# Low parts of the second weights on VectorE, and result buffers in fixed turns, in an attention and mixture-of-experts kernel

## The chip, the cores and the metric

The program runs on one core of a Trainium2 chip. The metric is the device time of one execution in microseconds (us), the median of several executions. Engine names in rows: PE is TensorE (PEld its weight loads), DVE is VectorE, ACT is ScalarE, POOL is GpSimd, SP is SyncE, which issues most of the DMAs.

## The reference

Causal attention over 8 batches, 8 heads, 576 positions and a head width of 64, with a bias from cumulated scores, gives x with 4608 rows (tokens) of 512 numbers. A mixture of 8 experts follows. Each token goes to one expert, and the expert's two products are what the change is about:

```python
logits = x @ w_gate
e_idx = np.argmax(logits, axis=1)
...
for e in range(E):
    mask = e_idx == e
    ...
    h = np.maximum(x[mask] @ w1[e], 0.0)
    ye = h @ w2[e]
    out[mask] = gate_w[mask, None] * eom[mask, e, None] * ye
```

x, w1 (8 x 512 x 1024), w2 (8 x 1024 x 512) and the output are float32.

## The kernel before, in words

**Attention** takes the first 350 us or so. A planner (class `Order`, L97) orders its tasks on all engines by a table of places; the end of it also begins expert 0: the low parts of expert 0's second weights are already made there (L970 to L979), by GpSimd or VectorE as the planner chooses. The change does not touch that.

**The experts** follow one after another, e = 0 to 7. Numbers are split for the products: every operand is kept as a high part (a rounded copy, made by ScalarE) and a low part (what is left of it, made by a subtraction), and each product is three matmuls: high by high, high by low, low by high.

- `split_w1(f)` (L745) makes, for the next expert, the high part of a block f of the first weights on ScalarE (L740) and the low part on VectorE (L743, `w1l<-w1r,w1h`), 128x512 each. There are 8 blocks.
- `split_w2(f)` (L1026) makes the parts of block f of this expert's second weights: high on ScalarE (L726), low by `w2_lo` (L729) on GpSimd. There are 8 blocks.
- `gemm1` (L785, matmuls at L794) makes block f of the hidden layer in a PSUM bank pair `ph`, of which there are two; `relu` (L798) reads it twice: ScalarE writes the high part `hh` (L804), VectorE the low part `hl` (L806). Block f + 2 needs the bank pair of block f, so TensorE can't begin it before `hl` of block f is done.
- `product2` (L827, matmuls at L832) is the second product of one tile of 128 tokens, in bank `py` or `pf`. `result` (L1054) multiplies it by the token's weight on VectorE into a buffer `y` (L1057), and `scatter` has GpSimd issue an indirect DMA that writes the rows to the output (L1031).
- `gemm2_few` (L1068) does the same for a last tile of 32 or 64 tokens, in plain float32, with its own y (L1084).
- `ready` (L1087) turns 128 gathered tokens of the next expert: transposes on TensorE (L771, bank `pt`, two of them), high part on ScalarE (L775), low part on VectorE (L779).

The number of tokens of an expert is known only at run time. So `front(e, C)` (L1090), the first product and the tiles beyond the fourth, is written out for nine counts C (512, 544, ... 768) as the arms of a switch (expert 0 has eighteen), and each engine jumps to the arm that fits. `back(e)` (L1167), what all arms share, follows: results of the first tile, the remaining tiles, and the `ready` calls of the next expert in between. In this run experts 0 to 7 take the arms 544, 512, 512, 672, 704, 512, 576 and 640. Arms 544 and 672 have a short tile of 32 tokens, 576 and 704 one of 64.

Inside an arm each engine's order is set by the framework's scheduler from dependencies; in `back` it is the order of the code. A pool gives the buffers: a tag with bufs=3 is handed out in rotation, and a tile that is taken must wait until the last use of its buffer is over. All y tiles, also the short tile's, came from one tag with three buffers.

Of the kernel before, what the change touches and what calls it, by code (L numbers as in the profile page):

```python
# [9 lines left out]
F32 = mybir.dt.float32  # L10
# [7 lines left out]
P = 128  # L18
# [175 lines left out]
def moe_attention(ctx, tc, qk, v, s, idg, w1, w2, out):  # L194
    nc = tc.nc
# [532 lines left out]
    def w2_lo(f, eng):  # L728
        eng.tensor_sub(w2f("l", f), w2r[:, f], w2f("h", f).bitcast(F32))  # L729
# [147 lines left out]
    def hint(e):  # L877
        tc.switch_hint({g: regs[e] for g in ENGINES}, (1 if e else 2) * NA, f"expert{e}")
# [146 lines left out]

    def split_w2(f):  # L1026
        w2_hi(f)
        w2_lo(f, nc.gpsimd)

    def place(dst, ix, y):  # L1030
        ins = nc.gpsimd.indirect_dma_start(  # L1031
            out=dst, out_offset=bass.IndirectOffsetOnAxis(ap=ix, axis=0), in_=y, in_offset=None,
            bounds_check=dst.shape[0] - 1, oob_is_err=False)
        tc.declare_no_dep(ins.ins, group="out", reason="every token has one expert")
        tc.add_to_no_dep_group("out", ins.ins)
# [4 lines left out]
    def ybank(tag):  # L1040
        return pm.tile([P, DM], F32, tag=tag, name=tag, bufs=1)

    def gemm2(e, t, C, between=((),), tag="py"):

        m = min(P, C - t * P)
        p = ybank(tag)
        n = NF // len(between)
        for k, steps in enumerate(between):
            for step in steps:
                step()  # L1050
            product2(t, m, p, range(k * n, (k + 1) * n))
        result(e, t, m, p)

    def result(e, t, m, p):  # L1054
        y = mw.tile([P, DM], F32, tag="y", name="y", bufs=3)
        tb = tbs[e % 2]
        nc.vector.tensor_scalar_mul(y[0:m], p[0:m], tb[0:m, t, 2:3])  # L1057
        scatter(y, tb, t, m)
# [9 lines left out]
    def gemm2_few(t, m, tb):  # L1068

        G = P // m  # L1070
        W = DM // G
        ix = mw.tile([P, 1], I32, tag="ixf", name="ixf", bufs=2)
        nc.vector.tensor_scalar(ix, tb.bitcast(I32)[:, 1:2], float(G), grp[m], ALU.mult, ALU.add)
        hf = wt["hf"][:, :, 0:m]
        sl = slice(t * P, t * P + m)
        for fs in (slice(0, 6), slice(6, NF)):
            nc.gpsimd.tensor_add(hf[:, fs], wt["hh"][:, fs, sl].bitcast(F32), wt["hl"][:, fs, sl].bitcast(F32))
        p = ybank("py")
        for f in range(NF):
            for g in range(G):  # L1080
                nc.tensor.matmul(p[g * m:(g + 1) * m, 0:W], hf[:, f], w2r[:, f, g * W:(g + 1) * W],  # L1081
                                 start=(f == 0), stop=(f == NF - 1))
        y = mw.tile([P, DM], F32, tag="y", name="y", bufs=3)
        nc.vector.tensor_scalar_mul(y[:, 0:W], p[:, 0:W], tb[:, 2:3])  # L1084
        place(out.rearrange("n (g w) -> (n g) w", g=G), ix, y[:, 0:W])

    def ready(t, xg):  # L1087
        xcopy(t, xtrans(xg, pm.tile([P, ND, P], F32, tag="pt", name="pt")))

    def front(e, C, early=False):  # L1090


        nxt = e + 1 < E
        T = (C + P - 1) // P
        few = C % P if C % P in grp else 0
        if e == 0 and not early:
            for t in range(ET):
                ready(t, gather(tbs[0], t, xgs[t]))
        if T > LT:
            ready(LT, wt["last"])  # L1100
        c0 = min(ET * P, C - 256) if early else 0
        if few:
            places = few_places(e, T - 1, few)
        if nxt and e > 0:
            load_tab(e + 1)
        if early:
            for t in range(EY):
                scatter(banks["ye", t], tbs[0], t, P)

        ahead = range(2) if T > LT and C - c0 > 512 else ()  # L1110
        ph = {}

        def block(f):
            ph[f] = pm.tile([P, 2, 512], F32, tag="ph", name="ph")
            return ph[f]

        for f in ahead:
            gemm1(f, c0, C, block(f), 0)
        for f in range(NF):
            if f in ahead:  # L1120
                gemm1(f, c0, C, ph[f], 1)
            else:
                gemm1(f, c0, C, block(f))
            for part in "hl":
                relu(f, c0, C, ph[f], part)
            if e > 0:
                split_w2(f)
            if nxt:

                if e > 0 or not early:  # L1130
                    split_w1(f)
                elif f > 1:
                    split_w1(f - 2)
                if f < TMAX:
                    gather(tbs[(e + 1) % 2], f, xgs[f])
        if nxt and e == 0 and early:
            for f in range(NF - 2, NF):
                split_w1(f)
        if not few and nxt:
            run_all(load_w2(e + 1))  # L1140
        if nxt and e + 2 < E:
            run_all(load_w1(e + 2))

        tiles = ([] if e or early else list(range(EY))) + list(range(NC, T))
        if few:
            tiles.insert(0, tiles.pop())
        first = 0 if e else ET
        f0 = 3 if few else 0
        if f0:
            product2(first, P, firsts[e], range(f0))  # L1150
        for k, t in enumerate(tiles):
            if few and k == 0:
                gemm2_few(t, few, places)
                if nxt:
                    run_all(load_w2(e + 1))
            else:
                gemm2(e, t, C)
            if k + 1 < len(tiles):
                product2(first, P, firsts[e], range(f0, f0 + 1))
                f0 += 1  # L1160
        product2(first, P, firsts[e], range(f0, FB))
# [5 lines left out]
    def back(e):  # L1167

        if e == 0:
            where = {EY: (("hint", 0, 1), (2,), (3,), (4,))}  # L1170
        else:
            where = {1: ((),), 2: ((0,), (1,)), 3: (("hint", 2), (3,), (4,), ())}
        first = 0 if e else ET
        product2(first, P, firsts[e], range(FB, NF))
        result(e, first, P, firsts[e])
        for t, parts in where.items():
            gemm2(e, t, CMAX, tag="pf" if e and t == 2 else "py", between=[[(lambda u=u: hint(e + 1) if u == "hint" else ready(u, xgs[u])) for u in part
                                if e + 1 < E] for part in parts])

    rest = nc.values_load(rgi[0:1, 2 * E:2 * E + 1], min_val=0, max_val=E * NOV,  # L1180
# [13 lines left out]
    with tc.If(rest > 0):  # L1194
        for e in range(E):
            rv = nc.values_load(rgi[0:1, E + e:E + e + 1], min_val=0, max_val=NOV,
                                skip_runtime_bounds_check_because="counted by comparisons")
            run_all(load_w1(e))
            run_all(load_w2(e))
            with tc.For_i(0, rv, 1) as it:  # L1200
                tb = mw.tile([P, 1, 3], F32, tag="tbo", name="tbo")
                nc.sync.dma_start(tb, tab[bass.ds(it * P + (e * N + CMAX), P), :].unsqueeze(1))
                xg = sh.tile([P, DM], F32, tag=XGS[0], name="xg", bufs=1)
                nc.gpsimd.indirect_dma_start(
                    out=xg, out_offset=None, in_=xd,
                    in_offset=bass.IndirectOffsetOnAxis(ap=tb.bitcast(I32)[:, 0, 0:1], axis=0),
                    bounds_check=N, oob_is_err=False)
                p = pm.tile([P, ND, P], F32, tag="pt", name="pt")
                for c in range(ND):
                    nc.tensor.transpose(p[:, c, :], xg[:, c * P:(c + 1) * P], ident)  # L1210
                xt = sh.tile([P, ND, P], F32, tag=XGS[1], name="xto", bufs=1)
                nc.vector.tensor_copy(xt, p)
                ho = sh.tile([P, NF, P], F32, tag="kq", name="ho")
                for f in range(NF):
                    p = pm.tile([P, 2, 512], F32, tag="ph", name="ph")
                    for c in range(ND):
                        nc.tensor.matmul(p[:, 0, 0:P], w1r[:, c, f * P:(f + 1) * P], xt[:, c, :],
                                         start=(c == 0), stop=(c == ND - 1))
                    nc.vector.tensor_scalar_max(ho[:, f, :], p[:, 0, 0:P], 0.0)
                p = ybank("py")  # L1220
                for f in range(NF):
                    nc.tensor.matmul(p, ho[:, f, :], w2r[:, f], start=(f == 0), stop=(f == NF - 1))
                y = mw.tile([P, DM], F32, tag="y", name="y", bufs=3)
                nc.vector.tensor_scalar_mul(y, p, tb[:, 0, 2:3])
                scatter(y, tb, 0, P)

# [56 lines left out]
```

## Time and profile before

| what | value |
|---|---|
| median of 3 runs | 812.53 us (811.99 to 815.26) |
| the profiled execution | 817.58 us |
| its span | 815.7 us |
| mean granted TensorE clock | 0.983 |
| busy: PE, DVE, ACT, POOL | 95%, 56%, 51%, 48% of the span |

The profiled execution is one execution, 5.05 us above the median of the runs; what lies around its span is 1.9 us. A granted clock of 1.00 is 2.4 GHz and one of 0.50 is 1.2 GHz. In the timelines a row gives its start from the beginning of the span, its time, the line and tile, and in brackets how long the engine stood idle before it and what ended that.

### The profile page before, as it was taken

To read this page: it belongs to the slowest core of one execution; us is meant where nothing else is said; L and a number is where in the kernel's file an instruction comes from. 1 tells how busy PE (TensorE), PEld (TensorE's weight loads), DVE (VectorE), ACT (ScalarE), POOL (GpSimd) and SP (SyncE) were. 2 spreads that over 40 slices of the span, in tenths; PEclk is the share of its full clock that TensorE was granted. 3 is DMA by queue.
4 is the path that set the end of the run, shared out by engine and by line. 5 is a ranking of instruction groups with operands and counts; after the bars stand their busy time and mean duration, and the time that the engine had idled before them with its cause. 6 is when DMAs were issued, how large, how long until landed. Compare 5 with 4: busy or idle time off the path is not lost.

```text
span 815.7 us, 15604 instructions
## 1 busy us (share of the span) xinstructions
PE 775.3 (95%) x5121; PEld 618.9 (76%) x5121; DVE 452.8 (56%) x1265; ACT 412.5 (51%) x1125; POOL 389.1 (48%) x637
## 2 busy tenths in 40 slices
PE   4899999999999999969889999999999999999996
PEld 2577777777777777659767888898888878978985
DVE  5577878787878788845426345352372363443211
ACT  4788888888888888631315152430431241421300
POOL 4644575666665665554516345271281172541501
PEclk9999999999999999969989999999999999999999
DMA  8977787989897886240562715326125127223001
GB/s 216 247 194 205 208 231 228 239 222 223 239 236 221 202 210 130 52 166 2 146 227 68 260 55 192 124 78 227 56 78 200 68 80 249 71 63 131 14 29 43
DMA packets 71152, 125.03 MB, mean 153 GB/s; under 512 B 13978, under 2 KB 32540, under 8 KB 70942
## 3 DMA queue, kind: packets, MB, share of 16 engines
q1 hardware_dynamic: 62862, 100.75, 44.1%
q0 software_dynamic: 8080, 22.08, 8.5%
q8 instruction: 58, 0.95, 0.5%
q14 instruction: 152, 1.25, 0.5%
HBM read 103.12 MB, written 19.82 MB: 151 GB/s over the span
## 4 chain that ended last, share of the span: by engine, by line
PE 79%; DMA 6%; issue 5%; another core or an unknown queue 3%; DVE 3%; POOL 2%; SPq 1%; ACT 1%; POOLq 0%; DVEq 0%; ACTq 0%
PE ph L794 20%; PE py L832 11%; PE PT L435 10%; PE A L483 9%; PE S L380 8%; PE pf L832 8%; PE M L513 5%; PE S L383 3%; PE pt L771 2%; DMA cb<-cum 2%; PE A L481 1%; PE py L1081 1%; DMA con<-in_con_dram 1%; DMA xg<-xd,tbe 1%
## 5 line engine op out<-in xcount | busy, mean ns | idle before, releaser
L1031 POOL DMA_INDIRECT out_dram<-y,tb x34 | 33.5, 985 | 180.7 <-DVE y L1057 173.5
L794 PE MATMUL ph<-xh,w1h 128*128 128x512 f32 (+6 forms) x312 | 104.3, 334 | 4.8 <-DVE hl L806 3.1
L794 PE MATMUL ph<-xl,w1h 128*128 128x512 f32 (+6 forms) x312 | 103.3, 331 | 0.2 <-DVE xl L779 0.2
L794 PE MATMUL ph<-xh,w1l 128*128 128x512 f32 (+6 forms) x312 | 103.0, 330 | 0.0
L435 PEld LDWEIGHTS PT<-con,e 128*128 128x128 f32 x768 | 83.7, 142 | 14.7 <-issue 9.3
L775 ACT CAST xh<-pt 128x512 fp32r<-128x512 f32 x37 | 21.6, 587 | 144.0 <-PE pt L771 138.1
L435 PE MATMUL PT<-con,e 128*128 128x128 f32 x768 | 92.5, 276 | 1.5 <-ACT e L422 0.6
L380 PE MATMUL S<-kq 64*128 64x384 f32 (+3 forms) x512 | 82.3, 451 | 4.8 <-DVE pt L339 2.9
L483 PE MATMUL A<-pt,vraw 128*64 128x448 f32 (+3 forms) x640 | 84.8, 411 | 0.0
L743 DVE TENSOR_TENSOR w1l<-w1r,w1h 128x512 fp32r<-128x512 f32 x46 | 52.8, 1152 | 53.2 <-ACT w1h L740 53.0
L380 PEld LDWEIGHTS S<-kq 64*128 64x128 f32 x512 | 48.9, 189 | 37.5 <-issue 12.5
L832 PE MATMUL py<-w,hh 128*128 128x512 f32 x240 | 76.4, 400 | 0.0
L339 DVE COPY pt<-PT 128x384 f32<-128x384 f32 (+3 forms) x161 | 73.4, 503 | 3.3 <-PE PT L435 2.5
L483 PEld LDWEIGHTS A<-pt,vraw 128*64 128x64 f32 x640 | 44.9, 137 | 39.0 <-issue 29.7
L794 PEld LDWEIGHTS ph<-xh,w1h 128*128 128x128 f32 x312 | 59.1, 189 | 11.1 <-issue 5.0
L422 ACT ACTIVATE e<-pbB,m 128x128 f32<-128x128 f32 (+1 forms) x128 | 64.6, 506 | 1.8 <-DVE m L394 1.6
L806 DVE SCALAR_TENSOR_TENSOR hl<-ph,hh 128x512 fp32r<-128x512 f32 (+6 forms) x72 | 50.3, 701 | 27.0 <-ACT hh L804 26.9
L729 POOL TENSOR_TENSOR w<-w2r,w 128x512 fp32r<-128x512 f32 x45 | 57.9, 1300 | 13.7 <-ACT w L726 7.2
L740 ACT CAST w1h<-w1r 128x512 fp32r<-128x512 f32 x48 | 29.7, 621 | 68.3 <-issue 53.7
L794 PEld LDWEIGHTS ph<-xl,w1h 128*128 128x128 f32 x312 | 59.2, 190 | 3.8 <-DVE xl L779 1.1
L794 PEld LDWEIGHTS ph<-xh,w1l 128*128 128x128 f32 x312 | 59.0, 189 | 2.9
L337 ACT COPY pt<-PT 128x512 f32<-128x512 f32 (+2 forms) x95 | 51.9, 580 | 16.4 <-PE PT L435 15.1
(167 smaller groups left out, 1706.0 us busy)
## 6 DMA issues: line engine op xcount, KB each, us to landing
kq<-in_qk_dram SPq DMA_DIRECT2D x32, 576.0 KB, 5.3
cb<-cumd SPq DMA_DIRECT2D x31, 512.0 KB, 7.2
w1r<-in_moe_w_dram SPq DMA_DIRECT2D x7, 2048.0 KB, 10.6
w2r<-in_moe_w_dram SPq DMA_DIRECT2D x7, 2048.0 KB, 10.0
vraw<-in_v_dram SPq DMA_DIRECT2D x32, 320.0 KB, 3.4
cb<-cum SPq DMA_DIRECT2D x62, 160.0 KB, 6.7
xd<-x SPq DMA_DIRECT2D x32, 256.0 KB, 4.7
w1r<-in_moe_w_dram SPq DMA_DIRECT2D x4, 512.0 KB
```

Source lines behind the costliest of these rows:

```text
L337: nc.scalar.copy(out, in_)
L339: nc.vector.tensor_copy(out, in_)
L380: nc.tensor.matmul(d["s", t, j][:, 0:width(t)], qt[js, t * P:(t + 1) * P], kt[js, j * TL:j * TL + width(t)], start=True, stop=True)
L422: nc.scalar.activation(e[:, o:o + W], pbias(i, t, j), AF.Exp, bias=st[i].pop(("m", t, j)), scale=-1.0, accum_out=sums[i % 3][:, j, t:t + 1])
L435: nc.tensor.transpose(p[:, (c * len(g) + n) * P:(c * len(g) + n + 1) * P], st[i][etile(t, j)][:, o:o + P], ident)
L483: nc.tensor.matmul(p[j * D:(j + 1) * D, OB + q0:OB + S], vt[:, j, c, :], pt[:, c, j, q0:S] if c < NM else d["ptl"][:, (1 - j) * D:(2 - j) ...
L513: nc.tensor.matmul(p[:, n * 2 * G2:(n + 1) * 2 * G2], o, idgt[:, i % NPAIR], start=True, stop=True)
L729: eng.tensor_sub(w2f("l", f), w2r[:, f], w2f("h", f).bitcast(F32))
L743: eng.tensor_sub(w1f("l", f), w1r[:, :, f * P:(f + 1) * P], w1f("h", f).bitcast(F32))
L794: nc.tensor.matmul(p[:, u, 0:W], w1f(a, f)[:, c, :], wt[b_][:, c, us], start=(n == 0), stop=(n == 3 * ND - 1))
L806: nc.vector.scalar_tensor_tensor(lv, pv, 0.0, hv.bitcast(F32), ALU.max, ALU.subtract)
L832: nc.tensor.matmul(p[0:m], wt[a][:, f, sl], w2f(b_, f), start=(f == 0 and n == 0), stop=(f == NF - 1 and n == 2))
```

## The change

`split_w2` makes its low parts on VectorE. `result` no longer takes its buffer in rotation but from one of three tags of one buffer each, y0 to y2, by a number that the caller gives: 0 for an expert's first tile, 1 and 2 in turn for the tiles in an arm, 1, 2, 0 for those in `back`. The short tile's result goes to a buffer of attention (tag e0) that nothing else uses by then.

```diff
@@ -1025,7 +1025,7 @@
 
     def split_w2(f):
         w2_hi(f)
-        w2_lo(f, nc.gpsimd)
+        w2_lo(f, nc.vector)
 
     def place(dst, ix, y):
         ins = nc.gpsimd.indirect_dma_start(
@@ -1040,7 +1040,7 @@
     def ybank(tag):
         return pm.tile([P, DM], F32, tag=tag, name=tag, bufs=1)
 
-    def gemm2(e, t, C, between=((),), tag="py"):
+    def gemm2(e, t, C, between=((),), tag="py", slot=0):
 
         m = min(P, C - t * P)
         p = ybank(tag)
@@ -1049,10 +1049,10 @@
             for step in steps:
                 step()
             product2(t, m, p, range(k * n, (k + 1) * n))
-        result(e, t, m, p)
-
-    def result(e, t, m, p):
-        y = mw.tile([P, DM], F32, tag="y", name="y", bufs=3)
+        result(e, t, m, p, slot)
+
+    def result(e, t, m, p, slot):
+        y = mw.tile([P, DM], F32, tag=f"y{slot}", name="y", bufs=1)
         tb = tbs[e % 2]
         nc.vector.tensor_scalar_mul(y[0:m], p[0:m], tb[0:m, t, 2:3])
         scatter(y, tb, t, m)
@@ -1080,9 +1080,9 @@
             for g in range(G):
                 nc.tensor.matmul(p[g * m:(g + 1) * m, 0:W], hf[:, f], w2r[:, f, g * W:(g + 1) * W],
                                  start=(f == 0), stop=(f == NF - 1))
-        y = mw.tile([P, DM], F32, tag="y", name="y", bufs=3)
-        nc.vector.tensor_scalar_mul(y[:, 0:W], p[:, 0:W], tb[:, 2:3])
-        place(out.rearrange("n (g w) -> (n g) w", g=G), ix, y[:, 0:W])
+        y = sh.tile([P, 256], F32, tag="e0", name="yf", bufs=1)[:, 0:W]
+        nc.vector.tensor_scalar_mul(y, p[:, 0:W], tb[:, 2:3])
+        place(out.rearrange("n (g w) -> (n g) w", g=G), ix, y)
 
     def ready(t, xg):
         xcopy(t, xtrans(xg, pm.tile([P, ND, P], F32, tag="pt", name="pt")))
@@ -1154,7 +1154,7 @@
                 if nxt:
                     run_all(load_w2(e + 1))
             else:
-                gemm2(e, t, C)
+                gemm2(e, t, C, slot=1 + (k - bool(few)) % 2)
             if k + 1 < len(tiles):
                 product2(first, P, firsts[e], range(f0, f0 + 1))
                 f0 += 1
@@ -1172,9 +1172,9 @@
             where = {1: ((),), 2: ((0,), (1,)), 3: (("hint", 2), (3,), (4,), ())}
         first = 0 if e else ET
         product2(first, P, firsts[e], range(FB, NF))
-        result(e, first, P, firsts[e])
-        for t, parts in where.items():
-            gemm2(e, t, CMAX, tag="pf" if e and t == 2 else "py", between=[[(lambda u=u: hint(e + 1) if u == "hint" else ready(u, xgs[u])) for u in part
+        result(e, first, P, firsts[e], 0)
+        for n, (t, parts) in enumerate(where.items()):
+            gemm2(e, t, CMAX, tag="pf" if e and t == 2 else "py", slot=(n + 1) % 3, between=[[(lambda u=u: hint(e + 1) if u == "hint" else ready(u, xgs[u])) for u in part
                                 if e + 1 < E] for part in parts])
 
     rest = nc.values_load(rgi[0:1, 2 * E:2 * E + 1], min_val=0, max_val=E * NOV,
@@ -1220,7 +1220,7 @@
                 p = ybank("py")
                 for f in range(NF):
                     nc.tensor.matmul(p, ho[:, f, :], w2r[:, f], start=(f == 0), stop=(f == NF - 1))
-                y = mw.tile([P, DM], F32, tag="y", name="y", bufs=3)
+                y = mw.tile([P, DM], F32, tag="y0", name="y", bufs=1)
                 nc.vector.tensor_scalar_mul(y, p, tb[:, 0, 2:3])
                 scatter(y, tb, 0, P)
```

The instructions of TensorE, ScalarE and SyncE stay in the order they had. VectorE's order changes, since the scheduler places the eight new subtractions. In these rows w20 to w27 (w2l4, w2l5) are blocks 0 to 7 of the second weights and w1l0 to w1l3 pairs of blocks of the first weights.

VectorE at the start of the 512 arm of expert 1, before:

```order
L1186 BRANCH_PREFETCH_HINT
L743 TENSOR_TENSOR w1l0_5742<-w1r_78,w1h0_5741 128x512
L806 SCALAR_TENSOR_TENSOR hl_5935<-ph_11967,hh_5934 128x512
L743 TENSOR_TENSOR w1l0_5742<-w1r_78,w1h0_5741 128x512
L806 SCALAR_TENSOR_TENSOR hl_5935<-ph_11989,hh_5934 128x512
```

and with the change:

```order
L1186 BRANCH_PREFETCH_HINT
L729 TENSOR_TENSOR w20_5864<-w2r_79,w20_5864 128x512
L729 TENSOR_TENSOR w21_5918<-w2r_79,w21_5918 128x512
L729 TENSOR_TENSOR w22_5857<-w2r_79,w22_5857 128x512
L729 TENSOR_TENSOR w23_5912<-w2r_79,w23_5912 128x512
L729 TENSOR_TENSOR w2l4_5874<-w2r_79,w2h4_5873 128x512
L729 TENSOR_TENSOR w2l5_5868<-w2r_79,w2h5_5867 128x512
L743 TENSOR_TENSOR w1l0_5742<-w1r_78,w1h0_5741 128x512
L806 SCALAR_TENSOR_TENSOR hl_5935<-ph_11967,hh_5934 128x512
L729 TENSOR_TENSOR w26_5942<-w2r_79,w26_5942 128x512
L729 TENSOR_TENSOR w27_5890<-w2r_79,w27_5890 128x512
```

Six of the eight now stand ahead of the first `hl`, and two ahead of the second.

VectorE at the start of the 672 arm of expert 3, before:

```order
L1073 TENSOR_SCALAR ixf_19907<-tbf_19628,grp32_103 128x1
L779 TENSOR_TENSOR xl_5840<-pt_19621,xh_5839 128x4x128
L743 TENSOR_TENSOR w1l0_5742<-w1r_78,w1h0_5741 128x512
L806 SCALAR_TENSOR_TENSOR hl_5935<-ph_19631,hh_5934 128x672
L743 TENSOR_TENSOR w1l0_5742<-w1r_78,w1h0_5741 128x512
```

and with the change:

```order
L729 TENSOR_TENSOR w20_5864<-w2r_79,w20_5864 128x512
L779 TENSOR_TENSOR xl_5840<-pt_19621,xh_5839 128x4x128
L729 TENSOR_TENSOR w21_5918<-w2r_79,w21_5918 128x512
L729 TENSOR_TENSOR w22_5857<-w2r_79,w22_5857 128x512
L729 TENSOR_TENSOR w23_5912<-w2r_79,w23_5912 128x512
L729 TENSOR_TENSOR w2l4_5874<-w2r_79,w2h4_5873 128x512
L729 TENSOR_TENSOR w2l5_5868<-w2r_79,w2h5_5867 128x512
L729 TENSOR_TENSOR w26_5942<-w2r_79,w26_5942 128x512
L729 TENSOR_TENSOR w27_5890<-w2r_79,w27_5890 128x512
L1073 TENSOR_SCALAR ixf_19907<-tbf_19628,grp32_103 128x1
L743 TENSOR_TENSOR w1l0_5742<-w1r_78,w1h0_5741 128x512
L806 SCALAR_TENSOR_TENSOR hl_5935<-ph_19631,hh_5934 128x672
```

All eight stand ahead of the first `hl`. The 704 arm of expert 4 reads the same with its own widths; in the 576 arm of expert 6 seven and in the 640 arm of expert 7 all eight stand directly ahead of the first `hl`.

VectorE at the start of `back(0)`, with what each row waits for, before:

```order
L1057 TENSOR_SCALAR y_11848<-pf_6243,tb0_96 128x512 [waits DMASW6_49,DMASW7_49,DMASW2_49,PE_49]
L878 SWITCH_STRIDE
L878 ISA
L878 BRANCH_PREFETCH_HINT
L779 TENSOR_TENSOR xl_5840<-pt_11894,xh_5839 128x4x128 [waits Activation_49]
L779 TENSOR_TENSOR xl_5840<-pt_11901,xh_5839 128x4x128 [waits Activation_49]
```

and with the change:

```order
L1057 TENSOR_SCALAR y_11848<-pf_6243,tb0_96 128x512 [waits PE_49]
L878 SWITCH_STRIDE
L878 ISA
L878 BRANCH_PREFETCH_HINT
L779 TENSOR_TENSOR xl_5840<-pt_11894,xh_5839 128x4x128 [waits Activation_49]
L779 TENSOR_TENSOR xl_5840<-pt_11901,xh_5839 128x4x128 [waits Activation_49]
```

The order is the same; the first result no longer waits for three queues of GpSimd's DMAs (DMASW).

## Rows read from the trace of the kernel before

**Rows 1.** Page, part 1: TensorE's busy time, share of the span and instructions.
```profile
PE 775.3 (95%) x5121; PEld 618.9 (76%) x5121; DVE 452.8 (56%) x1265; ACT 412.5 (51%) x1125; POOL 389.1 (48%) x637
```

**Rows 2.** TensorE's timeline in expert 0's second half: start, us, line, operation, tile, [idle before].
```profile
416.89 0.40 PE L832 MATMUL py<-w,hl 128*128 128x512 f32 x1
...
421.30 1.11 PE L771 MATMUL pt<-con,xg 128*128 128x128 f32 x4 [4.01 <-DVE xl L779]
...
429.16 0.39 PE L794 MATMUL ph<-xh,w1h 128*128 128x512 f32 x1
```

**Rows 3.** VectorE's timeline, the same stretch.
```profile
411.48 0.35 DVE L1084 TENSOR_SCALAR y<-py,tbf 128x128 f32<-128x128 f32 x1 [1.19 <-PE py L1081]
...
419.90 0.75 DVE L1057 TENSOR_SCALAR y<-pf,tb 128x512 f32<-128x512 f32 x1 [8.07 <-DMA out_dram<-y,ixf]
```

**Rows 4.** Windows of 1 us: PE, PEld, DVE, ACT, POOL busy, PEclk, DMA share, GB/s.
```profile
419.00:420.00 1.00, 0.00 (x0) 0.00 (x0) 0.10 (x1) 0.00 (x0) 0.00 (x0) 0.72 1.05 406
...
423.00:424.00 1.00, 1.00 (x4) 0.73 (x3) 0.69 (x1) 0.09 (x1) 0.00 (x0) 0.50 0.58 229
...
426.00:427.00 1.00, 1.00 (x5) 0.81 (x4) 0.51 (x1) 0.46 (x1) 0.00 (x0) 0.87 0.09 25
```

**Rows 5.** Chain of work in order of time: start, us, engine, tile, line, count.
```profile
429.32 10.90 PE ph L794 x48
440.29 11.36 PE ph L794 x48
...
475.79 21.99 PE ph L794 x96
...
515.51 1.40 PE py L832 x6
517.35 1.39 PE py L832 x6
...
538.44 14.99 PE ph L794 x96
...
651.31 22.19 PE ph L794 x96
```

**Rows 6.** TensorE's timeline: the other three idle stretches behind VectorE after 421.30.
```profile
538.44 0.39 PE L794 MATMUL ph<-xh,w 128*128 128x336 f32 x1 [0.41 <-DVE hl L806]
...
610.41 0.40 PE L794 MATMUL ph<-xh,w1h 128*128 128x352 f32 x1 [1.39 <-DVE hl L806]
...
721.62 0.37 PE L794 MATMUL ph<-xh,w1h 128*128 128x288 f32 x1 [1.73 <-DVE hl L806]
```

**Rows 7.** VectorE's timeline in expert 4, one low part of a first weight.
```profile
605.76 3.70 DVE L743 TENSOR_TENSOR w<-w1r,w 128x512 fp32r<-128x512 f32 x1 [2.02 <-ACT w L740]
```

**Rows 8.** GpSimd's timeline beside it.
```profile
606.37 2.54 POOL L729 TENSOR_TENSOR w<-w2r,w 128x512 fp32r<-128x512 f32 x2
```

**Rows 9.** VectorE's timeline where experts 2, 3, 4, 6 and 7 begin.
```profile
475.83 0.75 DVE L1057 TENSOR_SCALAR y<-py,tb 128x512 f32<-128x512 f32 x1 [1.45 <-PE py L832]
479.08 0.69 DVE L743 TENSOR_TENSOR w1l<-w1r,w1h 128x512 fp32r<-128x512 f32 x1 [2.50 <-ACT w1h L740]
479.69 0.68 DVE L806 SCALAR_TENSOR_TENSOR hl<-ph,hh 128x512 fp32r<-128x512 f32 x1
...
525.36 0.21 DVE L1073 TENSOR_SCALAR ixf<-tbf,grp 128x1 int32<-128x1 int32 x1 [2.63 <-issue]
...
587.86 0.22 DVE L1073 TENSOR_SCALAR ixf<-tbf,grp 128x1 int32<-128x1 int32 x1 [2.42 <-issue]
...
701.07 0.21 DVE L1073 TENSOR_SCALAR ixf<-tbf,grp 128x1 int32<-128x1 int32 x1 [2.65 <-issue]
...
753.04 0.75 DVE L1057 TENSOR_SCALAR y<-py,tb 128x512 f32<-128x512 f32 x1 [1.45 <-PE py L832]
```

**Rows 10.** ScalarE's timeline where experts 2 and 7 begin.
```profile
473.90 2.18 ACT L726 CAST w<-w2r 128x512 fp32r<-128x512 f32 x4 [0.24 <-ACT xh L775]
...
753.44 1.14 ACT L726 CAST w<-w2r 128x512 fp32r<-128x512 f32 x2 [2.57 <-issue]
```

## The prediction, made before the changed kernel ran

> **What bounds the kernel now.** I read the page first: TensorE is busy for 95% of the span [rows 1], so only what shortens or lengthens its idle time can count. Then TensorE's timeline from expert 0's second half on, looking for idle stretches and what ended them. There are four behind VectorE: 4.01 us before 421.30 [rows 2], and 0.41, 1.39 and 1.73 us in experts 3, 4 and 6 [rows 6]. VectorE's own long waits elsewhere in `back` (some for a scatter, in experts 3 and 4) leave no gap on TensorE; they cost nothing.
>
> The 4.01 us begin with the y buffer. The short tile's result is made at 411.48 and scattered; expert 0's first result needs a buffer again and waits 8.07 us, to 419.90, until that scatter has landed [rows 3]. VectorE works in order, so the low parts of the gathered tokens stand behind it, their bank `pt` is not freed, and TensorE stops at 417.29 (416.89 plus 0.40). It then also loses its clock: 0.72 of full speed in the microsecond from 419, 0.50 at 423, 0.87 from 426 [rows 4]. Read as time at 1.2 GHz, that is from about 419.4 to 426.3.
>
> The three smaller stretches come from GpSimd. In expert 4 VectorE starts a low part of a first weight at 605.76 and takes 3.70 us [rows 7]; the same work takes 0.69 us elsewhere [rows 9]. GpSimd runs two subtractions from 606.37 to 608.91 [rows 8], and VectorE ends 0.55 us after them: it got nothing done beside them. `hl` stands behind that, and TensorE behind `hl`. The 512 arms show the same weakly: expert 1's first four blocks take 10.90 us, its last four 11.36; experts 2 and 5 take 21.99 and 22.19 for eight, against twice 10.90 [rows 5]. That is 0.46, 0.19 and 0.39 us.
>
> **The change, part by part.** *Fixed turns and the short tile's own buffer.* The first result of expert 0 waits for TensorE alone. What was held up from 417.1 on (the next issue after 416.89) are three steps of four transposes and six matmuls. At full clock a step takes 1.84 us (515.51 to 517.35) [rows 5], three take 5.5. Before, expert 1 began at 429.16 [rows 2], 12.06 us after 417.1. The gain is **6.5 us**: 4.0 of idle time, 2.5 of clock. What is late next is small: token parts are ready about as TensorE asks for them.
>
> *Low parts on VectorE.* Eight subtractions of 128x512 per expert, 56 in all. Back to back one takes 0.61 us (479.08 to 479.69) [rows 9], so 56 take 34 us. VectorE is idle 44% of the span, and the 1.3 to 3.7 us that first-weight parts take beside GpSimd fall to 0.69. In the middle of an arm this is hidden and the waits of rows 5 and 6 go. The cost is at the arm's start, where they stand ahead of the first `hl`; TensorE waits there when it comes to its third block.
>
> Expert 2 (512 arm): VectorE's last result ends at 476.58 (475.83 plus 0.75) [rows 9]. I take 0.24 us to enter the arm, as ScalarE shows there [rows 10]. Six parts, a first-weight part and `hl` follow: 476.8 plus 3.66, 0.61 and 0.68 is 481.8. The third block is due two blocks of 2.73 after 475.79, at 481.2; with 0.1 for the signal it waits 0.66 us. Later `hl` are in time. Net of what rows 5 give back: +0.47 in expert 2, +0.27 in expert 5, +0.20 in expert 1. Expert 1 has a second cost: it starts 6.5 us sooner, at 422.6, but its second weights are still loading; the DMA engines are at 0.58 in the microsecond from 423 and at 0.09 from 426 [rows 4]. That adds 0 to 1.6 us; I take 0.7, for most of the traffic is over by 424.
>
> Expert 3 (672 arm): VectorE enters late, at 525.36, with 2.63 us for which nothing is named [rows 9]. Ten instructions of 0.61 (the token part counted as one), 0.15 for the index and about 0.85 for a wider `hl` (estimate, from 0.68 for 512) end at 532.5. The third block starts 0.1 later, the fifth two blocks on. A block takes 3.68 (14.99 for four, less the last one's tail of 0.28) [rows 5]: 539.9 against 538.44 before [rows 6], **+1.5**.
>
> Expert 4 (704): from 587.86 [rows 9] the same to 595.1; four blocks of 3.85 (3.68 by width) bring the seventh to 610.5 against 610.41: +0.1. Its old stall of 1.39 is spent at the front. Expert 6 (576): from 701.07 [rows 9] seven parts and `hl` end at 706.1, five blocks of 3.15 later it is 721.95 against 721.62 [rows 6]: +0.3.
>
> Expert 7 (640) had no such work on VectorE. Its last result there ends at 753.79 [rows 9]. If it enters as ScalarE did, 2.57 us later [rows 10], eight parts and `hl` end at 762.1, and the third block, due at 760.0 (two blocks of 3.50), waits **2.1 us**. If it enters at once, ScalarE's high parts set the pace and nothing is lost. Late entry is what VectorE shows in the other three long arms, so I take 2.1.
>
> Nothing else moves on the path: the loads of the second weights can be issued sooner, the gathers too, and both have slack.
>
> **Sum.** -6.5 (expert 0) +0.9 (1) +0.5 (2) +1.5 (3) +0.1 (4) +0.3 (5) +0.3 (6) +2.1 (7) is **-0.8 us**: 816.8 against 817.58 for the profiled execution. That stands 5.05 us above the median; taken off, the median becomes **811.7**, which is no change, since about 0.5% (4.1 us) is what a measurement of this kernel can tell.
>
> **The rivals.** *Late entry in the 512 arms too (slower).* VectorE's entry there is hidden: its first row at 479.08 waited 2.50 us for ScalarE [rows 9], so entry may take anything up to that. If it takes 2.5, each front starts 2.3 us later: +6.8 over three arms, less the 0.7 that expert 1 has counted already: 811.7 plus 6.1 is 817.8. It decides from about 0.9 us of extra entry per arm. Against it speak ScalarE's 0.24 us in that arm and that it stands directly behind the switch; for it, 2.4 to 2.6 us in three of the seven. The Trainium skill, "Runtime: NRT & Kernel Launch", section "Instruction fetch mechanics", says that a taken branch to code outside the prefetched window must fetch it before going on; by that rule longer arms on VectorE, as here, would speak for this rival, and the trace agrees for the long arms and leaves the 512 arm open. Chance 0.15.
>
> *Entry is quick everywhere (faster).* If VectorE's late rows were not the jump, the parts would start some 2.5 us sooner in experts 3, 4, 6 and 7; then nothing is lost there and the 0.41, 1.39 and 1.73 us of rows 6 are won: -6.5 +1.7 (the 512 arms) -3.5 is -8.3, 804.2. Three like rows marked with no releaser speak against it. 0.08. Only expert 7 quick: -2.9, 809.6, still no change. 0.12.
>
> *The clock falls in a new wait.* By the sums above TensorE now waits 1.9 to 2.3 us at one place in each of experts 3, 4, 6 and 7. An idle stretch of 1.73 [rows 6] cost no clock; the one of 4.01 cost it about 2.1 us in, and then 6.9 us at half speed [rows 4]. A fall would cost up to 3.4: 815.1 for one, 818.5 for two. 0.14.
>
> *The change does not do what it says:* expert 0's result finds another wait, such as tokens or weights that land no sooner. Then the 6.5 stay: 818.2. The row's remaining wait names only TensorE, against it. 0.05.
>
> **How the numbers follow.** The forecast, with small errors of a term, has 0.40; 0.06 is for what I have not seen. Faster by over 0.5% (under 808.5) takes the quick entry and the low edges of the forecast and of expert 7: 0.20. Slower (over 816.6) takes late entry, the failed change and two falls of the clock: 0.23. The rest, 0.57, is no change. The range 806.0 to 818.5 leaves out most of the quick entry and the ends beyond two falls; the forecast's own is 809 to 814.
>
> **What would show it.** Right: no idle stretch of TensorE at 417 and a clock of 1.00 there; first-weight parts at 0.69 us throughout; a single wait of TensorE behind `hl` at the third block of each expert, about 0.7 us in the 512 arms and 2 us in the others, and none later. Wrong: waits of 2 us or more in the 512 arms, a clock of 0.50 inside an arm, no wait at all at third blocks, or the idle stretch in expert 0 still there.

## The result: slower by 0.8%, and where the time went

The changed kernel takes 820.39 us (median of 6 runs, 818.49 to 823.47) against 814.12 for the kernel before on the same chip: a ratio of 1.0083, 95% interval 1.0059 to 1.0107. A second comparison (below) gave 1.0105. The forecast was 811.7, its range ended at 818.5. In two of the four later sets of runs the kernel before took 834 and 840 us instead of 813 to 815, with expert 0's short tile at 430 to 441 us of the profiles instead of 408 to 414, so every ratio below is to the kernel before in the same set.

The short tile's result of expert 0 starts at 411.48 before [rows 3] and at 409.04 after. A second profile of the changed kernel has it at 413.54, so this difference is chance, and time is best counted from there, by the starts of VectorE's results `y`. To the last `y` of the kernel it is 396.9 us before and 405.5 after, 8.6 more (the second profile has 402.5, 5.6 more):

| stretch, us | before | after | difference | forecast |
|---|---|---|---|---|
| expert 0, short tile's result to last `y` | 17.9 | 17.6 | -0.3 | -6.5 |
| expert 1, last `y` to last `y` | 46.5 | 46.9 | +0.4 | +0.9 |
| expert 2 | 46.2 | 46.9 | +0.8 | +0.5 |
| expert 3 | 62.7 | 64.0 | +1.3 | +1.5 |
| expert 4 | 66.6 | 66.8 | +0.2 | +0.1 |
| expert 5 | 46.3 | 46.9 | +0.5 | +0.3 |
| expert 6 | 55.4 | 57.2 | +1.9 | +0.3 |
| expert 7, to its first `y` | 33.6 | 37.4 | +3.8 | +2.1 |

TensorE's busy time stays at 95% of a longer span; GpSimd's falls from 389.1 us [rows 1] to 314.0. The page after:

```profile
PE 777.2 (95%) x5121; PEld 622.0 (76%) x5121; DVE 455.0 (55%) x1321; ACT 412.3 (50%) x1125; POOL 314.0 (38%) x581
```

The larger group of low parts of first weights on VectorE follows, for the kernel before and then for the changed one (count | busy us, mean ns of one). The 0.69 us forecast for one is there; that part of the change works.

```profile
L743 DVE TENSOR_TENSOR w1l<-w1r,w1h 128x512 fp32r<-128x512 f32 x46 | 52.8, 1152 | 53.2 <-ACT w1h L740 53.0
```
```profile
L743 DVE TENSOR_TENSOR w1l<-w1r,w1h 128x512 fp32r<-128x512 f32 x46 | 32.1, 700 | 48.3 <-ACT w1h L740 48.3
```

TensorE's timeline after shows these idle stretches over 0.4 us: expert 0's, and one at the third block of each expert (experts 1 and 5 have the 0.71 of expert 2, and expert 3 has 1.53).

```profile
418.06 1.12 PE L771 MATMUL pt<-con,xg 128*128 128x128 f32 x4 [3.24 <-DVE xl L779]
...
479.62 0.47 PE L794 MATMUL ph<-xh,w1h 128*128 128x512 f32 x1 [0.71 <-DVE hl L806]
...
595.02 0.40 PE L794 MATMUL ph<-xh,w1h 128*128 128x352 f32 x1 [1.44 <-DVE hl L806]
...
706.46 0.40 PE L794 MATMUL ph<-xh,w1h 128*128 128x288 f32 x1 [2.04 <-DVE hl L806]
...
764.37 0.41 PE L794 MATMUL ph<-xh,w1h 128*128 128x320 f32 x1 [2.02 <-DVE hl L806]
```

The stretch of 4.01 us [rows 2] is still there, at 3.24, one of the prediction's own signs of being wrong. The others sit where the forecast put them, and the late waits of [rows 6] are gone. What the forecast's sum left out is in the windows (columns as in [rows 4]; PEclk is the third number from the end): the clock falls to 0.50 (1.2 of 2.4 GHz) in expert 0, and again after the waits of experts 6 and 7.

```profile
417.00:418.00 1.00, 0.00 (x0) 0.00 (x0) 1.00 (x3) 0.00 (x0) 0.31 (x1) 0.63 1.05 406
418.00:420.00 2.00, 1.94 (x7) 1.74 (x8) 0.73 (x3) 0.59 (x1) 0.69 (x1) 0.50 1.07 399
420.00:424.00 4.00, 4.00 (x13) 3.22 (x12) 1.26 (x2) 0.59 (x1) 0.00 (x0) 0.50 0.40 145
...
706.00:708.00 2.00, 1.54 (x9) 1.54 (x10) 2.00 (x5) 0.00 (x0) 1.59 (x2) 0.85 0.44 129
708.00:710.00 2.00, 2.00 (x10) 2.00 (x10) 1.00 (x2) 0.00 (x0) 1.50 (x2) 0.50 0.50 141
710.00:712.00 2.00, 2.00 (x14) 2.00 (x14) 0.00 (x0) 0.63 (x2) 1.51 (x2) 0.80 0.73 186
...
764.00:766.00 2.00, 1.63 (x9) 1.63 (x10) 1.05 (x2) 0.00 (x0) 0.00 (x0) 0.86 0.00 0
766.00:768.00 2.00, 2.00 (x10) 2.00 (x9) 0.00 (x0) 0.00 (x0) 0.00 (x0) 0.50 0.00 0
768.00:770.00 2.00, 2.00 (x13) 2.00 (x13) 0.00 (x0) 0.23 (x1) 0.00 (x0) 0.79 0.00 0
```

Expert 6 loses 0.30, 1.00 and 0.40 us of full clock in its three windows, 1.7 in all; expert 7 0.28, 1.00 and 0.42, again 1.7. These are the 1.6 and 1.7 by which both exceed their forecasts. In the second profile of the changed kernel only expert 7 of the two loses clock.

**Expert 0.** VectorE's timeline shows a wait of 7.28 us where 8.07 stood [rows 3], although the result now waits for no scatter:

```profile
409.04 0.35 DVE L1084 TENSOR_SCALAR yf<-py,tbf 128x128 f32<-128x128 f32 x1 [1.19 <-PE py L1081]
416.66 0.75 DVE L1057 TENSOR_SCALAR y<-pf,tb 128x512 f32<-128x512 f32 x1 [7.28 <-issue]
```

The rows of the sequencers (a q behind the engine's name; by line, with first and last start at the end) tell what the timeline doesn't: each engine's branch at the arm's end, and its first instruction behind it, a register load (L874) or, on SyncE, a move. The register loads wait for no semaphore.

```profile
L1279 SPq COMPARE_BRANCH  x2: 50/54/58, 409.5 to 416.5; - x2
L1279 SPq MOVE  x2: 38/40/41, 416.2 to 416.3; - x2
...
L1279 DVEq COMPARE_BRANCH  x1: 56/56/56, 409.1 to 409.1; - x1
L1279 POOLq COMPARE_BRANCH  x1: 49/49/49, 409.4 to 409.4; - x1
```
```profile
L874 DVEq TENSOR_LOAD <-rgi x1: 317/317/317, 416.2 to 416.2; - x1
L874 POOLq TENSOR_LOAD <-rgi x1: 317/317/317, 416.3 to 416.3; - x1
```

Three engines leave the arm between 409.1 and 409.5 and start behind it within 0.1 us of each other, some 7 us later (GpSimd's engine still works on the scatter until 410.7). In between, the queues that load instructions move nothing from 409 to 412, while the 4 MB of weights issued at the arm's end hold the DMA engines; then the packets of those queues run, and the engines go on. The DMA views of 409 to 412 and of 412 to 415 (packets, MB, share):

```profile
q1 hardware_dynamic: 227, 0.93, 93.7%
```
```profile
q1 hardware_dynamic: 266, 1.02, 94.2%
...
q14 instruction: 4, 0.03, 2.8%
q8 instruction: 1, 0.02, 2.2%
```

The same register load was in the trace of before, and the prediction did not read it:

```profile
L874 DVEq TENSOR_LOAD <-rgi x1: 314/314/314, 418.0 to 418.0; - x1
```

Before, then, VectorE was out of the arm at 418.3 only (418.0 plus 0.3), and the scatter held it from there to 419.90: 1.6 us of the 8.07.

### The profile page after: what moved, and what is told of

The parts are those of the page before. It is cut to its first block, busy times and chain, and to the rows that moved or that the text cites. A ratio compares the mean times of both kernels' runs of the same rounds, so it can differ in the third digit from the quotient of the medians.

```text
span 821.6 us, 15585 instructions
## 1 busy us (share of the span) xinstructions
PE 777.2 (95%) x5121; PEld 622.0 (76%) x5121; DVE 455.0 (55%) x1321; ACT 412.3 (50%) x1125; POOL 314.0 (38%) x581
## 5 line engine op out<-in xcount | busy, mean ns | idle before, releaser
L380 PEld LDWEIGHTS S<-kq 64*128 64x128 f32 x512 | 49.3, 191 | 39.8 <-issue 13.1
L804 ACT ACTIVATE hh<-ph 128x512 fp32r<-128x512 f32 (+6 forms) x72 | 43.7, 609 | 31.2 <-PE ph L794 26.9
L743 DVE TENSOR_TENSOR w1l<-w1r,w1h 128x512 fp32r<-128x512 f32 x46 | 32.1, 700 | 48.3 <-ACT w1h L740 48.3
```

What stands on the lines that cost most here:

```text
L380: nc.tensor.matmul(d["s", t, j][:, 0:width(t)], qt[js, t * P:(t + 1) * P], kt[js, j * TL:j * TL + width(t)], start=True, stop=True)
L743: eng.tensor_sub(w1f("l", f), w1r[:, :, f * P:(f + 1) * P], w1f("h", f).bitcast(F32))
L804: nc.scalar.activation(hv, pv, AF.Relu)
```

## The experiments

Theory J says that expert 0's wait is the jump out of the arm, slow because code is fetched while weights load, and that the scatter's wait runs beside it. Theory B, as predicted, says that it is the buffer. Theory Q says that in the other experts the loss is the place of the low parts ahead of the first `hl`; its rival W, that it is the work itself.

**The fixed turns alone.** The low parts go back: `w2_lo(f, nc.vector)` becomes `w2_lo(f, nc.gpsimd)` in `split_w2`.

> The fixed turns and the short tile's own buffer alone; the low parts stay on GpSimd. Theory J (VectorE and the sequencers of GpSimd and SyncE are held at the jump from the arm to the code behind it, whose code they must fetch while 4 MB of weights load): before, VectorE's register load behind that jump began at 418.0, so the buffer held the result only from 418.3 to 419.9, 1.6 us of the 8.07. The wait in front of expert 0's first result falls from 8.1 to about 6.5 us, TensorE's idle time behind it from 4.0 to 2.4 to 3.3 us with the clock still at 0.50 for some us, and the total is 1 to 2 us under before: 812 to 813, ratio 0.998 to 0.999. Theory B (the buffer was the whole wait, as predicted): no idle time and full clock there, 807.6, ratio 0.992.

811.65 us, ratio 0.9975 (0.9951 to 0.9999). In this profile the jump took 5.5 us (the short tile's result ends at 408.67, the register load starts at 414.1), TensorE was idle for 1.85 us, less than expected, and the clock still fell to 0.50. B falls, for its 0.992 lies outside the interval; J's 0.998 to 0.999 lies inside.

**The low parts alone.** The kernel before with `w2_lo(f, nc.vector)`.

> The low parts on VectorE alone; the result buffers rotate by three as before. Theory J: expert 0 is as before (4.0 us idle), all of the loss is in the arms, so this is the changed kernel plus the 1 to 2 us of the buffer: 820.5 to 822.5, ratio 1.008 to 1.010. Theory B: the changed kernel plus 6.5 is 827, ratio 1.016.

822.37 us, 1.0091 (1.0072 to 1.011): J's range again, and B's 1.016 lies outside. TensorE's idle time was 3.14 us, not 4.0.

**The kernel before, expert 0's loads behind the arm.**

```
     def front(e, C, early=False):
-        if not few and nxt:
+        if not few and nxt and e:
             run_all(load_w2(e + 1))
-        if nxt and e + 2 < E:
+        if nxt and e and e + 2 < E:
             run_all(load_w1(e + 2))
...
-                if nxt:
+                if nxt and e:
                     run_all(load_w2(e + 1))
...
     def back(e):
         first = 0 if e else ET
+        if e == 0:
+            run_all(load_w2(1))
+            run_all(load_w1(2))
         product2(first, P, firsts[e], range(FB, NF))
```

> The kernel before with one edit: the 4 MB of weights that expert 0's arm loads at its end are issued behind the arm, by the code that follows the switch. Theory J: with no load under way the jump takes about 2.5 us, as the entries into the long arms do (2.4 to 2.7 us with little traffic), the short tile's scatter lands sooner too, expert 0's first result starts by 415, TensorE is not idle at 417 and keeps a clock of 1.00: 6.5 us are won, of which expert 1 gives 0 to 3 back because its second weights land 4 to 6 us later; 807.5 to 811, ratio 0.992 to 0.996. Rival J2 (the jump takes its 6 to 7 us with or without traffic): the wait stays over 6 us, nothing is won, and the later weights cost 0 to 5 us; 814 to 819, ratio 1.000 to 1.006.

813.77 us, 0.9987 (0.9969 to 1.0004). For the total this is a miss of J, and J2's 1.000 lies inside the interval; the trace decides. VectorE's timeline and its register load:

```profile
411.29 0.35 DVE L1084 TENSOR_SCALAR y<-py,tbf 128x128 f32<-128x128 f32 x1 [1.19 <-PE py L1081]
418.91 0.75 DVE L1057 TENSOR_SCALAR y<-pf,tb 128x512 f32<-128x512 f32 x1 [7.27 <-DMA out_dram<-y,ixf]
```
```profile
L874 DVEq TENSOR_LOAD <-rgi x1: 318/318/318, 414.1 to 414.1; - x1
```

The jump fell to 2.5 us (411.64 to 414.1), so J2 falls. But now the buffer is the later of the two: 4.5 us from 414.4 to 418.9. The scatter did not land by 415; the weights issued behind the arm are under way with it.

**Both: the turns, and expert 0's loads behind the arm**, low parts on GpSimd.

> The fixed turns and the later loads together, low parts on GpSimd. Theory J: the buffer no longer matters when the scatter lands at once; within 1 us of the run with the later loads alone, ratio 0.992 to 0.996. If the buffer is what remains in that run, this one is 1 us or more faster than it. Rival J2: as the turns alone, or slower by the later weights, ratio 0.998 to 1.006.

811.17 us, 0.9957 (0.9941 to 0.9973), 2.6 us under the run without the turns. The two intervals just overlap, but the trace shows too that the buffer is what remained in that run. VectorE's timeline, its register load and TensorE's timeline:

```profile
412.58 0.75 DVE L1057 TENSOR_SCALAR y<-pf,tb 128x512 f32<-128x512 f32 x1 [3.25 <-PE pf L832]
```
```profile
L874 DVEq TENSOR_LOAD <-rgi x1: 320/320/320, 412.0 to 412.0; - x1
```
```profile
416.39 0.63 PE L771 MATMUL pt<-con,xg 128*128 128x128 f32 x4 [1.60 <-DMA out_dram<-yf,ixf]
```

Only with both gone does the result wait for TensorE. The clock is 1.00 throughout, and expert 0 takes 13.1 us. The packets of the instruction queues now run in 409 to 412, while little of the weights moves:

```profile
q1 hardware_dynamic: 156, 0.32, 55.3%
q8 instruction: 1, 0.02, 2.2%
q14 instruction: 2, 0.02, 1.7%
```

The edit moves less than its name says: SyncE, already behind the arm, issues one 2 MB load at 409.0, where the changed kernel issues one too, and the other at 409.5 instead of 407.5.

What is left of TensorE's idle time, 1.60 us, the row puts down to the short tile's scatter, and TensorE's sequencer agrees. GpSimd issues the scatter at 409.61, it lands 6.6 us later, and the last of the three semaphore instructions on the transposes' line (the last start, 416.3) stands right behind that:

```profile
409.61 1.03 POOL L1031 DMA_INDIRECT out_dram<-yf,ixf  x1 [1.42 <-DVE yf L1084]
...
out_dram<-yf,ixf POOLq DMA_INDIRECT x1, 6.6
...
L771 PEldq EVENT_SEMAPHORE  x3: 51/51/51, 410.2 to 416.3; - x3
```

In the kernel before and in the changed one the same row reads:

```profile
L771 PEldq EVENT_SEMAPHORE  x3: 51/51/51, 413.1 to 419.7; - x3
```
```profile
L771 PEldq EVENT_SEMAPHORE  x3: 51/51/51, 410.1 to 417.1; - x3
```

The scatter landed at 419.7 and at 417.0 there, and in all sixteen profiles the row stands within 0.05 us behind the landing. So three waits ran side by side: jump, buffer and TensorE's own for the scatter. Of the 4.01 us before, jump and buffer alone decided the last 1.5 (419.8 to 421.30). The rows do not tell which dependency makes TensorE wait for the scatter, and no run takes this wait away.

The jump in all profiles, from the end of the short tile's result to VectorE's register load, and expert 0's length:

| kernel | jump | result held by | TensorE idle | expert 0 |
|---|---|---|---|---|
| before | 6.2 | jump, then buffer | 4.01 | 17.9 |
| changed, two profiles | 6.9, 6.0 | jump | 3.24, 2.40 | 17.6, 15.3 |
| turns alone | 5.5 | jump | 1.85 | 15.0 |
| low parts alone | 6.0 | jump, then buffer | 3.14 | 16.3 |
| before, loads behind the arm | 2.5 | buffer | 3.24 | 16.2 |
| turns, loads behind the arm | 2.7 | neither | 1.60 | 13.1 |

The further profiles below agree: 5.3 us twice where the loads stay in the arm, 2.4 to 3.2 in seven where they don't.

**The low parts pinned.** The changed kernel, each low part kept behind what is written ahead of it on VectorE, the `hl` of its block.

```
-        eng.tensor_sub(w2f("l", f), w2r[:, f], w2f("h", f).bitcast(F32))
+        return eng.tensor_sub(w2f("l", f), w2r[:, f], w2f("h", f).bitcast(F32))
...
-        w2_lo(f, nc.vector)
+        tc.keep_in_program_order(w2_lo(f, nc.vector))
```

> The changed kernel with one edit: each low part of a second weight stands on VectorE right behind the hl of its block, instead of six to eight of them ahead of the first hl. Same work, same engines, nothing else moves on VectorE or ScalarE. Theory Q (the loss is the queue: the low parts in front of the first hl make TensorE wait at its third block, 0.71 us three times, 1.53, 1.44, 2.04 and 2.02 us, and after the two waits of 2 us the clock falls, some 1.6 us more each): the waits and the clock loss go, 8 to 12 us, so 808 to 812, ratio 0.992 to 0.997 to the kernel before; expert 0 stays as in the changed kernel, with some 3 us idle. Rival W (it is the work itself, 34 us more on VectorE, wherever it stands): the waits only move to later blocks, 818 to 821, ratio 1.004 to 1.008.

0.9955 (0.9928 to 0.9982), and once more:

> The run with pinned parts alone, once more. Theory Q: 0.991 to 0.996, that is 1.2 to 1.7% under the changed kernel's 1.0083; expert 0 with some 3 us idle and the clock at 0.50 for some us, experts 1, 2 and 5 at 45.9 to 46.5 us and expert 7's arm at 33.6 us, as in the kernel before. Rival W: 1.000 or more.

0.9961 (0.993 to 0.9992). VectorE does the same work (455.2 us against 455.0), and from the short tile's result to the last `y` it is 389.7 and 390.3 us, against 405.5 and 402.5 in the two profiles of the changed kernel. W falls, since its range began at 1.004. Of the waits at third blocks only expert 1's is left (0.32 and 0.90 us), and late in expert 6 there is one of 1.68 and 1.24 us, behind a late high part of ScalarE and not behind low parts. Not all of the gain is the pinning's, for expert 0 took 13.2 us in both, where it was expected to stay as it was. The jump still takes 5.3 us, but the token part behind it is done only 0.2 to 0.3 us after the scatter has landed, so TensorE's own wait covers it:

```profile
439.72 0.66 PE L771 MATMUL pt<-con,xg 128*128 128x128 f32 x4 [1.64 <-DVE xl L779]
```

This idle time did not cost the clock (1.00 in both), while the 1.85 us of the turns alone did. Without expert 0 the comparison is 376.5 and 377.1 us against 387.9 and 387.2, and 379.1 in the kernel before; so Q holds.

Expert 7's start on VectorE, in the first of the two profiles, shows the new order: the parts stand between the `hl`, which wait for ScalarE alone.

```profile
772.14 0.83 DVE L806 SCALAR_TENSOR_TENSOR hl<-ph,hh 128x640 fp32r<-128x640 f32 x1 [4.81 <-ACT hh L804]
772.88 0.68 DVE L729 TENSOR_TENSOR w<-w2r,w 128x512 fp32r<-128x512 f32 x1
774.41 0.82 DVE L806 SCALAR_TENSOR_TENSOR hl<-ph,hh 128x640 fp32r<-128x640 f32 x1 [0.84 <-ACT hh L804]
```

In the changed kernel the same place reads, from its first low part to its first two `hl`:

```profile
758.68 2.50 DVE L729 TENSOR_TENSOR w<-w2r,w 128x512 fp32r<-128x512 f32 x4 [2.58 <-ACT w2h L726]
761.10 1.28 DVE L729 TENSOR_TENSOR w2l<-w2r,w2h 128x512 fp32r<-128x512 f32 x2
762.30 1.28 DVE L729 TENSOR_TENSOR w<-w2r,w 128x512 fp32r<-128x512 f32 x2
763.50 1.54 DVE L806 SCALAR_TENSOR_TENSOR hl<-ph,hh 128x640 fp32r<-128x640 f32 x2
```

**Pinned, and expert 0's loads behind the arm**, twice.

> The same with the loads of expert 0's arm issued behind the arm. Theory Q with J: 3 to 5 us under the run without the later loads (expert 0 neither idle nor at half clock), 803.5 to 808, ratio 0.986 to 0.992. Rival W: 814 to 818. If the second weights of expert 1 land too late for VectorE's low parts, expert 1 takes 1 us or more longer than in the run without the later loads.

> The run with pinned parts and expert 0's loads moved, once more, since its first interval was 0.991 to 0.997 wide. Theory Q with J: 0.986 to 0.994; on a profile without the stall in expert 4's arm, TensorE idle under 4 us in all from 400 us on, against 7.5 in the kernel before.

0.9941 (0.9909 to 0.9973) and 0.9949 (0.9919 to 0.9978): no further gain that the intervals can tell, and both lie just above what was expected. Expert 0 takes 13.0 and 12.9 us, but it took 13.2 with the loads in the arm, so there was almost nothing to win in it. Expert 4 holds a stall of TensorE of 2.81 and of 1.05 us at the end of its arm, with nothing named.

**The changed kernel, expert 0's loads behind the arm.**

> The changed kernel with the loads of expert 0's arm issued behind the arm, low parts in front as in the change. Theory J: what the buffer edit was predicted to give now shows: VectorE is behind the jump some 2.5 us after it, no idle time of TensorE at 417, clock 1.00; 3.5 to 5 us under the changed kernel, 815.5 to 817.5, ratio 1.002 to 1.005. If the jump were not what held it: 820 to 822, ratio 1.008 to 1.011.

1.0093 (1.0059 to 1.0128), a miss. By the total it fits the other theory (1.008 to 1.011), but in its trace expert 0 takes 13.1 us at full clock. The changed kernel was not run in that set, so both follow once more, side by side:

> The changed kernel itself, on the same chip as the next two. Theory: 1.006 to 1.011, as in its first comparison, with expert 0 from the short tile's result to its last one at 16 to 18 us, experts 6 and 7 with a wait of 2 us each and a clock of 0.50 after it.

> The changed kernel with expert 0's loads behind the arm, beside the changed kernel on one chip. Theory J: expert 0 takes 13.1 us instead of 16 to 18, and the total is 3 to 5 us (0.4 to 0.6%) under the changed kernel. If what is won in expert 0 is given back elsewhere, as the ratio of 1.0093 in the first run of it suggests, the two are within 1.5 us and the trace shows where.

1.0105 (1.0073 to 1.0137) and 1.0079 (1.0052 to 1.0106), 822.48 and 820.67 us: 1.8 us less where 3 to 5 were expected, and the intervals overlap. The traces agree with the smaller figure: the changed kernel's expert 0 took 15.3 us here, not 17.6, and 13.1 with the loads moved. Expert 6 waited 2.20 us in this profile of the changed kernel and kept its clock, which was not expected either.

**All experts' loads behind their arms**, with pinned parts twice, and once with the low parts on GpSimd. In `front` the three lines that load are left out; in `back`:

```
+        if e + 1 < E:
+            run_all(load_w2(e + 1))
+        if e + 2 < E:
+            run_all(load_w1(e + 2))
         product2(first, P, firsts[e], range(FB, NF))
```

> The low parts pinned behind the hl of their block, and in every expert the loads of the next weights issued behind the arm instead of at its end. Theory Q with J: no engine crosses the jump out of an arm under a load, so besides expert 0's wait the stalls of TensorE's own sequencer at the end of expert 4's arm go too (1.2 and 2.8 us in the two runs with only expert 0's loads moved, put down to nothing that the profile shows). 1 to 3 us under the run with the pinned parts and expert 0's loads moved: ratio 0.984 to 0.991. If late weights matter (they now land 5 to 8 us later in each expert, in a stretch behind the arm of 22 us), waits for w1r or w2r appear on ScalarE at the start of the next arm and it is no faster: 0.990 to 0.996.

> The same loads and the fixed turns, with the low parts on GpSimd as before. Theory J: 0 to 2 us under the run with only expert 0's loads moved, ratio 0.993 to 0.996; the waits behind GpSimd's subtractions (1.4 us in expert 4, 1.6 in expert 6) stay. The distance to the run with pinned parts is what low parts on VectorE are worth when they stand behind the hl: 3 to 5 us by the idle rows that go.

> The best version so far, with a narrower interval: 0.986 to 0.992 to the kernel before, 1.7 to 2.2% under the changed kernel of the same call.

0.9891 (0.9839 to 0.9942) pinned, 0.9932 (0.9904 to 0.9961) on GpSimd, and pinned again 0.9893 (0.9851 to 0.9934): 805.77 us against 813.41, beside 822.48 for the changed kernel in the same set. It beats both of these. Against the version on GpSimd, where the wait of 1.43 us in expert 4 stayed as expected but the one in expert 6 did not, the intervals overlap. In the last run TensorE has one idle stretch left over 0.3 us from 400 us on, the one behind the scatter. Page and TensorE's timeline of that run:

```profile
PE 771.9 (96%) x5121; PEld 617.9 (77%) x5121; DVE 456.9 (57%) x1321; ACT 412.7 (51%) x1125; POOL 314.0 (39%) x581
```
```profile
419.45 0.63 PE L771 MATMUL pt<-con,xg 128*128 128x128 f32 x4 [1.50 <-DMA out_dram<-yf,ixf]
```

## Why the prediction was wrong, point by point

- **Expert 0, -6.5: the step that failed.** "The 4.01 us begin with the y buffer" and "The first result of expert 0 waits for TensorE alone". The row named the scatter because it landed last, 1.6 us after VectorE came out of the jump; the jump alone keeps most of the wait. Measured: 0.3 won in the first profile, 2.6 in the second, and by the ratio 2.0 us of the total for the turns alone. The rival "The change does not do what it says" (818.2) is what happened, at a chance of 0.05; its argument, "The row's remaining wait names only TensorE", read the program's semaphores and forgot the branch ahead of them. Even with both waits gone expert 0 falls by 4.8 us, not 6.5: 1.4 to 1.6 us of idle time stay at the same transposes, TensorE's own wait for the scatter, which the prediction put at nothing.
- **Its mechanism stood in the prediction, at the wrong place.** The Trainium skill, "Runtime: NRT & Kernel Launch", section "Instruction fetch mechanics", says that a taken branch out of the prefetched window stops for a DMA fetch. I weighed that for the entry into arms (2.42 to 2.65 us, [rows 9, 10]) and not for the exit, where the fetch meets 4 MB of weights. The traces agree that the jump stops. That it stops longer beside other traffic is not on that page but in the traces: 2.4 to 3.2 us with those loads later, 5.3 to 6.9 with them under way.
- **Late entry in the 512 arms (rival).** It did not come: VectorE enters expert 2 after 0.28 us, experts 3, 4, 6 and 7 after 2.49 to 2.67, as the forecast had it.
- **Waits at third blocks: right.** 0.71 us in the 512 arms (forecast 0.66), 2.02 in expert 7 (2.1); experts 1 to 5 come to +3.2 us against a forecast of +3.3. That they agree to 0.1 is partly luck: expert 1 is 0.5 under its term, since no wait for the loading second weights came, and experts 2 and 5 are 0.2 to 0.3 over theirs.
- **The clock: the second step that failed.** The sum took the falls as a rival of 0.14 because a stretch of 1.73 us had cost no clock. Two came in the first profile, in experts 6 and 7, at 1.7 us each, and one in the second. The rival's "up to 3.4" was twice what these cost: each lasted 3.4 us at half speed instead of the 6.9 that it took from expert 0.
- **Sum.** -0.8 was forecast; 6.2 not won in expert 0, 3.3 in experts 6 and 7 against their terms and -0.1 in the others make the +8.6 of the first profile; the medians moved by 6.3. Another 1.6 us of the miss are the starting point: the kernel before measured 814.12 here, and the forecast started from 812.53. The range ended at 818.5 because it added neither rival to the other.

Still open is which dependency makes TensorE wait for the scatter, and how much of the 6.5 us would come without it. That the moved loads gained so little in the pinned kernel fits expert 0's 13.2 us there, but no run tells by how much. That TensorE's stalls at the end of expert 4's arm are fetches was argued, not shown: they are absent from all three profiles with all loads moved, but the kernel before has none either.

## What to carry to other kernels

A row names the releaser that came last; before a wait is priced, look for the engine's own sequencer rows, which say whether it had arrived at all. Waits that run side by side give little until all of them are gone; here there were three. Work moved to an idle engine is cheap only behind what the bottleneck asks of that engine first, and large loads are better issued behind a jump than ahead of it.

## What the runs showed of the hardware

- With 4 MB of weights loading, VectorE, GpSimd and SyncE all took some 7 us from the arm to the code behind it in the changed kernel. VectorE took 5.3 to 6.9 us in the seven profiles with those loads and 2.4 to 3.2 us in the nine where they were issued later; GpSimd, counted from the same result, 6.4 to 6.9 and 4.5 to 5.2.
- The short tile's scatter took 6.4 to 7.6 us from issue to landing in all sixteen profiles, whether the loads were early or late.
- Waits of nearly one length did and did not cost the clock. Expert 7's, 1.99 to 2.16 us, cost it in all five profiles that have low parts ahead of `hl`; expert 6's cost it in two (2.04 us both) and not in three (2.06 to 2.20, granted clock 1.00 after). The price of a fall times its chance is the honest term here, and it should have been in the sum.
